# Sliding-window attention feeding a gated MLP: probabilities times values in plain float32, and GpSimd's subtractions and ScalarE's scalings moved to VectorE

## The chip, the cores and the metric

The kernel runs on one core of one Trainium2 chip. The metric is device time in microseconds (us) of one launch. Engines are named as in the profile: PE is TensorE's matmul, PEld its weight load, DVE is VectorE, ACT is ScalarE, POOL is GpSimd, SP is SyncE, which issues most of the DMAs.

## The reference

Three stages follow each other. Attention has batch 2, 8 heads, 768 positions and head size 64, a window of 128 positions and 4 sink positions; the result is laid out as 1536 tokens by 512 channels and goes through a two-layer MLP of width 2048. The third stage applies top-1 experts to the tokens whose score `x @ w_skip` is positive.

```
scores = where(is_sink | in_window, q @ k.T / sqrt(D), -1e9)
a = exp(scores - max);  a = a / (sum(a) + 1e-9);  attn = a @ v
h = x @ w_in
g = where(h >= 1, h, where(h <= -1, 0, (h + 1)**2 / 4))
x = g @ w_out
out = x;  out[x @ w_skip > 0] += gate * (relu(xc @ w1[e]) @ w2[e])
```

With the inputs used here no token has a positive score, so the kernel reads the weights of no expert and ends after a test of the scores. The MLP's weights come as float64 and are turned into float32 in the kernel.

## The kernel before, in words

**Precision.** Most products run on float32r, a rounded float32. To keep float32 accuracy each operand is split into a high part (rounded to float32r) and a low part (what the rounding left, by a subtraction), and a product is the sum of three matmuls: high times high, low times high, high times low. This holds for the scores, for probabilities times values, and for both layers of the MLP.

**Attention.** The work is cut into 48 units, in the order batch, group of 256 queries (3 per batch), head; two neighbouring heads are a pair, of which there are 24. Eight pairs lie in a first group (g = 0) and have no sinks of their own; the other 16 do. For a unit, `score` (line 385) makes the masked scores of two tiles of 128 queries in PSUM, takes their maximum on DVE (line 397) and the exponential with its sum on ACT (line 401). `norm` (line 406) adds 1e-9 to the sums on POOL (line 410), takes the reciprocal on DVE (line 411), and scales the first tile on ACT (line 418) and the second on DVE (line 416). `ptrans` (line 429) turns the blocks of 128 by 128 on PE into PSUM (line 443; 3 blocks where g = 0, else 4), from which ACT writes the high part `pth` (line 448) and DVE the low part `ptl` (line 449). `av` (line 460) multiplies them with the values of the pair and adds the sinks' share; ACT and DVE then write the high and low parts of the result (lines 485 and 486).

**Values.** `load_v` (line 289) loads the values of four heads into `vn` through SP's queue; `split_v` (line 310) splits them per pair into `vst`, which holds three blocks of 128 keys: the high part by ACT for the first 4 pairs (line 317), by DVE for the other 20 (line 319), the low part by POOL for all 24 (line 320). The matmuls of a pair at line 480 are these:

```
mm = [(1, 0, 256, 0), (2, 128, 128, 2)]                    # g == 0
mm = [(1, 0, 256, 0), (2 or 0, 0, 128, 2), (0 or 2, 128, 128, 3)]
for kb, c0, w, i0 in mm:
    for x, pp in ((0, pthp), (1, pthp), (0, ptlp)):
        todo.append((oj[:, :, c0:c0 + w], vs[:, x, kb], pp[:, :, ...]))
```

Each covers both heads of the pair, so w = 256 is a matmul of 512 columns and w = 128 one of 256 columns.

**MLP.** A unit of the MLP is 256 tokens by 256 hidden channels: 24 matmuls of 256 columns (`h_mm`, line 493), the activation (`h_act`, lines 505 to 529: ACT, ACT, DVE, ACT, and the low part `gl` on an engine given by the caller), and 12 matmuls of 512 columns (`y_mm`, line 531). 15 units run beside the attention in pieces; the rest follow in `behind` (line 582). Weights are converted by `conv` (line 201): three or more bit operations on DVE (lines 172 to 174), the high part on ACT (line 180), the low part by `lower` (line 183). 12 conversions are made by `conv` beside the attention, with the low part on POOL, the other 20 in `behind`, with the low part on DVE.

**Order.** In the attention the order on PE is written out by hand: for each step `s_` a string such as `aq.A.k.bPs.` (line 722) says when scores (a, b), transposes of q, k and probabilities (q, k, P, s), probabilities times values (A) and MLP pieces (a dot) go. The order on the other queues is chosen by a planner at build time. In `behind` the order of all engines is written by hand. Of queues, SP carries the loads of q, k, v and of the raw weights, the swaps of halves of the transposed queries (lines 349 and 350) and the partial results.

Of the kernel before, what the change touches and what calls it, by code (L numbers as in the profile page):

```python
# [8 lines left out]
F32 = mybir.dt.float32  # L9
F32R = mybir.dt.float32r  # L10
# [14 lines left out]
def attention_moe_skip_kernel(  # L25
# [15 lines left out]
    nc = tc.nc  # L41
# [72 lines left out]


    kts = [ap.tile([P, 3 * (P + SK)], F32R, name=f"kt{h}", bufs=1) for h in range(H)]
    vst = [ap.tile([P, 2, 3, P], F32R, name=f"vst{i}", bufs=1) for i in range(NP)]
    pcs = [ap.tile([P, 2, 72], F32R, name=f"pc{i}", bufs=1) for i in range(2)]
    ones = const.tile([P, 1], F32, name="ones")
    nc.vector.memset(ones, 1.0)  # L120
# [80 lines left out]
    def conv(w, f, wp, ranged):  # L201
        t = wp.tile([P, 2, 512], F32R, name="wi" if w == 0 else "wo")
        cf = bits(raws.pop((w, f)), ranged)
        upper(cf, t[:, 0])
        lower(cf, t[:, 0], t[:, 1], nc.gpsimd)
        (woh if w else wih)[f] = t


# [56 lines left out]
    natqk, natv, pr_, st = {}, {}, [dict() for _ in range(NPR)], [dict() for _ in range(NU)]  # L265

    def geo(n):

# [18 lines left out]
        natqk[m] = (qn, kn)  # L287

    def load_v(m):
        b, g, h0, kbs, _ = geo(4 * m)  # L290
        vn = ap.tile([P, 2, 4, D], F32, name="vn")
        for t in range(2):
            r = kbs[t] * P
            nc.sync.dma_start(vn[:, t], v[b, h0:h0 + 4, r:r + P, :].rearrange("h p d -> p h d"))
        natv[m] = vn

    def split_qk(u):
        qn, kn = natqk[u // 2]
# [11 lines left out]
    def split_v(u):  # L310
        b, g, h, kbs, s0 = geo(2 * u)
        vn = natv[u // 2]
        i = 2 * (u % 2)
        vs = vst[h // 2]
        vv = vs.rearrange("p x k (j d) -> p x k j d", j=2)[:, :, s0:s0 + 2]
        if u < 4:
            nc.scalar.activation(vv[:, 0], vn[:, :, i:i + 2], AF.Copy)
        else:
            nc.vector.tensor_copy(vv[:, 0], vn[:, :, i:i + 2])
        nc.gpsimd.tensor_tensor(out=vv[:, 1], in0=vn[:, :, i:i + 2], in1=vv[:, 0].bitcast(F32), op=ALU.subtract)  # L320
        pr_[u].update(vs=vs)
# [84 lines left out]
    def norm(n):  # L406
        g = units[n][1]
        pr, lsum = st[n]["pr"], st[n]["lsum"]
        rs = ap.tile([P, 2], F32, name="rs", bufs=3)
        nc.gpsimd.tensor_scalar(out=rs, in0=lsum, scalar1=1e-9, scalar2=None, op0=ALU.add)  # L410
        nc.vector.reciprocal(rs, rs)  # L411
        for t in range(2):
            w = span_of(n, t)[1]
            a, r = pr[:, t, :w], rs[:, t:t + 1]
            if t:
                nc.vector.tensor_scalar(out=a, in0=a, scalar1=r, scalar2=None, op0=ALU.mult)  # L416
            else:
                nc.scalar.activation(a, a, AF.Copy, scale=r)
        if g:

            j = SK * (n % 2)
            pc = pcs[n // 2 % 2]
            dst = pc.rearrange("p t (x c) -> p t x c", x=9)[:, :, 0::8, j:j + SK]
            src = pr[:, :, P:P + SK]
            nc.gpsimd.tensor_copy(dst, src.unsqueeze(2).to_broadcast([P, 2, 2, SK]))
            nc.gpsimd.tensor_tensor(
                out=pc[:, :, 32 + j:32 + j + SK], in0=src, in1=pc[:, :, j:j + SK].bitcast(F32), op=ALU.subtract)

    def ptrans(n):

        g = units[n][1]
        pr = st[n]["pr"]
        lo_, hi_ = 0, P + SK
        if g == 0:
            blocks = [(0, 0), (1, lo_), (1, hi_)]
        elif g % 2:
            blocks = [(0, lo_), (1, hi_), (0, hi_), (1, lo_)]
        else:
            blocks = [(0, hi_), (1, lo_), (0, lo_), (1, hi_)]
        w = len(blocks) * P  # L440
        pt = pst.tile([P, 512], F32, name="pt")
        for i, (t, c) in enumerate(blocks):
            nc.tensor.transpose(pt[:, P * i:P * i + P], pr[:, t, c:c + P], ident)  # L443
        pr = pr_[n // 2]
        if n % 2 == 0:
            pr.update(pth=ap.tile([P, 2, 512], F32R, name="pth", bufs=1), ptl=ap.tile([P, 2, 512], F32R, name="ptl", bufs=1))
        pth, ptl = pr["pth"][:, n % 2, :w], pr["ptl"][:, n % 2, :w]
        nc.scalar.activation(pth, pt[:, :w], AF.Copy)  # L448
        nc.vector.tensor_tensor(out=ptl, in0=pt[:, :w], in1=pth.bitcast(F32), op=ALU.subtract)  # L449
# [9 lines left out]

    def av(u):  # L460
        b, g, h, _, _ = geo(2 * u)
        vs = pr_[u]["vs"]
# [10 lines left out]
        pthp, ptlp = pr_[u]["pth"], pr_[u]["ptl"]  # L473
        for kb, c0, w, i0 in mm:
            for x, pp in ((0, pthp), (1, pthp), (0, ptlp)):
                todo.append((oj[:, :, c0:c0 + w], vs[:, x, kb], pp[:, :, i0 * P:i0 * P + w]))
        if g:
            todo.append((oj, vsk[b][:, h // 2], psk[0:72].unsqueeze(1).to_broadcast([72, 2, 256])))
        for i, (out_, lhs, rhs) in enumerate(todo):
            nc.tensor.matmul(out_, lhs, rhs, start=(i == 0), stop=(i == len(todo) - 1))  # L480
        gi = b * NG + g
        hp = h // 2
        for j in range(2):
            r = slice(D * j, D * j + D)
# [160 lines left out]

# [51 lines left out]
    with tc.manual_schedule(engines={mybir.EngineType.PE}):  # L697
        for s_ in range(-1, NU + 1):
# [25 lines left out]
            for what in order:  # L724
                if what == ".":
                    a, b = np_ * dot // dots, np_ * (dot + 1) // dots
                    dot += 1
                    for i in range(b - a):
                        pieces[done["piece"]]()
                        done["piece"] += 1  # L730
                elif what == "q":
                    upto("tq", done["tq"] + 1, NPR, trans_q)
                elif what == "k":
                    if s_ >= 0:
                        upto("tk", done["tk"] + 1, NU, lambda n: trans_k(n // 2, n % 2))
# [149 lines left out]
    def general_mlp(gp):  # L885
# [5 lines left out]
        for f in range(0, NF, 2):  # L891
# [154 lines left out]
```

## Time and profile before

| | |
|---|---|
| median of 3 runs | 446.63 us (445.97 to 447.99) |
| the profiled execution's own time | 449.18 us |
| its span, first to last instruction | 447.4 us |
| mean granted TensorE clock | 0.943 of full |
| PE / PEld busy | 393.0 (88%) / 354.1 (79%) us |
| DVE / ACT / POOL busy | 328.6 (73%) / 261.0 (58%) / 101.4 (23%) us |
| attention and the MLP beside it | 0 to 246 us |
| MLP alone | 246 to about 439 us |

The profile has one execution. A group is the instructions of one line, engine and shape, with the mean duration of one. A matmul's duration is a model and neighbouring matmuls overlap in it: what one really costs in a row of matmuls is read from the difference of start times. The chain of work that ended last is followed back from the last instruction, at each step to what released it. Of a SyncE wait the profile names the engine that released it last.

### The profile page before, as it was taken

The numbers are of one execution on the slowest core, as the hardware profiler recorded it, in microseconds if no ns is written. First come the engines' busy times: TensorE is split into PE (matmuls) and PEld (weight loads), VectorE is DVE, ScalarE is ACT, GpSimd is POOL, SyncE is SP. The second block draws the span as 40 slices with busy tenths as digits, with TensorE's granted clock in tenths as the row PEclk, the third lists the DMA queues.
The fourth block names the chain that finished last, engine by engine and source line by source line (L and its number), as shares of the span: only waits on it lengthen the run. The fifth ranks groups of instructions, "written<-read, shape, count | busy, mean of one in ns | idle before, by whom it ended". The sixth has DMA issues, their size and how long they took to land.

```text
span 447.4 us, 7553 instructions
## 1 busy us (share of the span) xinstructions
PE 393.0 (88%) x2476; PEld 354.1 (79%) x2476; DVE 328.6 (73%) x823; ACT 261.0 (58%) x625; POOL 101.4 (23%) x223
## 2 busy tenths in 40 slices
PE   4576566999899989999999999999999999999970
PEld 4565465998788878888889979999999999999950
DVE  6999999467788878888885689878854875444452
ACT  3766656688788869898797455444433333333310
POOL 6386566334322323233222000000000000000000
PEclk9966669899999989999999999999999999999995
DMA  6796575322424334241120256544325896555131
GB/s 152 206 282 164 142 211 144 92 50 47 120 48 95 106 87 96 53 112 25 26 72 5 66 188 206 181 132 142 111 79 188 284 347 217 189 188 189 47 141 58
DMA packets 69089, 59.12 MB, mean 132 GB/s; under 512 B 41008, under 2 KB 57392, under 8 KB 69040
## 3 DMA queue, kind: packets, MB, share of 16 engines
q1 hardware_dynamic: 67952, 58.28, 44.5%
q8 instruction: 22, 0.36, 0.4%
q10 hardware_dynamic: 1088, 0.26, 0.3%
q14 instruction: 27, 0.22, 0.2%
HBM read 46.47 MB, written 6.29 MB: 118 GB/s over the span
## 4 chain that ended last, share of the span: by engine, by line
PE 62%; DVE 17%; ACT 9%; issue 5%; DMA 3%; POOL 2%; ACTq 0%; POOLq 0%; DVEq 0%; SPq 0%
PE ph L500 15%; PE y L545 13%; PE z L545 12%; PE pt L500 10%; PE pt L480 5%; PE sc L395 3%; ACT pr L401 2%; DVE xl L486 2%; PE pt L443 2%; DVE cc L174 2%; DVE pr L397 2%; DVE ptl L449 1%; DVE pr L416 1%; DVE cc L173 1%; ACT pth L448 1%
## 5 line engine op out<-in xcount | busy, mean ns | idle before, releaser
L500 PE MATMUL ph<-xh,wi 128*128 128x256 f32 x496 | 93.3, 288 | 3.1 <-DVE rs L411 2.8
L500 PEld LDWEIGHTS ph<-xh,wi 128*128 128x128 f32 x496 | 79.1, 193 | 5.7 <-issue 3.0
L545 PE MATMUL y<-wo,gh 128*128 128x512 f32 x224 | 71.5, 400 | 1.2 <-ACT mr L564 1.2
L500 PE MATMUL ph<-xl,wi 128*128 128x256 f32 x248 | 70.9, 286 | 1.7 <-DVE xl L486 1.7
L500 PEld LDWEIGHTS ph<-xl,wi 128*128 128x128 f32 x248 | 48.4, 195 | 2.3 <-DVE xl L486 2.3
L395 PE MATMUL sc<-kt,qt 128*128 128x260 f32 (+1 forms) x192 | 47.0, 336 | 3.6 <-DMA qt<-qt 2.3
L401 ACT ACTIVATE pr<-pr,negmax 128x260 f32<-128x260 f32 (+1 forms) x96 | 46.7, 487 | 5.3 <-DVE negmax L397 4.3
L522 ACT ACTIVATE gh<-mt 128x512 fp32r<-128x512 f32 x48 | 30.3, 631 | 33.1 <-PE z L545 13.2
L545 PE MATMUL z<-wo,gh 128*128 128x512 f32 x160 | 49.2, 389 | 0.0
L500 PE MATMUL pt<-xh,wi 128*128 128x256 f32 x272 | 48.8, 281 | 0.0
L545 PEld LDWEIGHTS y<-wo,gh 128*128 128x128 f32 x224 | 39.7, 190 | 7.7 <-ACT mr L564 1.4
L545 PE MATMUL y<-wo,gl 128*128 128x512 f32 x112 | 43.9, 392 | 0.0
L500 PEld LDWEIGHTS pt<-xh,wi 128*128 128x128 f32 x272 | 42.7, 188 | 1.3
L395 PEld LDWEIGHTS sc<-kt,qt 128*128 128x128 f32 x192 | 35.2, 222 | 6.1 <-issue 1.9
L528 DVE TENSOR_TENSOR gl<-mt,gh 128x512 fp32r<-128x512 f32 x33 | 22.9, 693 | 23.1 <-ACT gh L522 23.0
L514 ACT ACTIVATE mt<-ph,half 128x512 f32<-128x512 f32 x31 | 21.3, 687 | 31.3 <-PE ph L500 31.2
L443 PE MATMUL pt<-ident,pr 128*128 128x128 f32 x176 | 30.9, 294 | 9.1 <-ACT kt L376 3.9
L500 PE MATMUL pt<-xl,wi 128*128 128x256 f32 x136 | 38.2, 281 | 0.0
L449 DVE TENSOR_TENSOR ptl<-pt,pth 128x512 fp32r<-128x512 f32 (+1 forms) x48 | 30.9, 643 | 7.7 <-ACT pth L448 7.2
L520 DVE SCALAR_TENSOR_TENSOR mt<-ph,mt 128x512 f32<-128x512 f32 x31 | 21.3, 688 | 18.6 <-ACT mt L515 16.9
L480 PE MATMUL pt<-pth,vst 128*128 128x256 f32 (+1 forms) x128 | 34.1, 356 | 0.0
L545 PEld LDWEIGHTS z<-wo,gh 128*128 128x128 f32 x160 | 28.8, 188 | 4.9
(119 smaller groups left out, 833.0 us busy)
## 6 DMA issues: line engine op xcount, KB each, us to landing
raw<-in_moe_w_in_dram SPq DMA_DIRECT2D x32, 512.0 KB, 4.5
raw<-in_moe_w_out_dram SPq DMA_DIRECT2D x32, 512.0 KB, 4.0
qt<-qt SPq DMA_DIRECT2D x44, 128.0 KB, 2.4
vn<-in_v_dram SPq DMA_DIRECT2D x24, 128.0 KB, 3.2
ypart<-mr SPq DMA_DIRECT2D x12, 256.0 KB, 3.0
yi<-ypart SPq DMA_DIRECT2D x12, 256.0 KB, 4.3
out_dram<-mr SPq DMA_DIRECT2D x12, 256.0 KB, 2.0
qn<-in_q_dram SPq DMA_DIRECT2D x22, 128.0 KB, 2.5
```

Of the source, the lines that this page charges most:

```text
L174: nc.vector.scalar_tensor_tensor(out=c, in0=L_, scalar=29, in1=c, op0=ALU.logical_shift_right, op1=ALU.bitwise_or)
L395: nc.tensor.matmul(sc[:, :w], qt[:, x, n % 2, P * t:P * t + P], kts[h][:, c0:c0 + w], start=(x == 0), stop=(x == 1))
L401: nc.scalar.activation(pr[:, t, :w], pr[:, t, :w], AF.Exp, bias=negmax[:, mi:mi + 1], scale=-1.0, accum_out=lsum[:, t:t + 1],)
L443: nc.tensor.transpose(pt[:, P * i:P * i + P], pr[:, t, c:c + P], ident)
L449: nc.vector.tensor_tensor(out=ptl, in0=pt[:, :w], in1=pth.bitcast(F32), op=ALU.subtract)
L480: nc.tensor.matmul(out_, lhs, rhs, start=(i == 0), stop=(i == len(todo) - 1))
L500: nc.tensor.matmul(ph, wih[f + i][:, wx, c * P:c * P + P], xx[gi][:, c], start=(c == 0 and x == 0), stop=(c == KC - 1 and x == 2),)
L514: nc.scalar.activation(t, ph, AF.Relu, bias=half, scale=0.5)
L520: nc.vector.scalar_tensor_tensor(out=t, in0=ph, scalar=1.0, in1=t, op0=ALU.max, op1=ALU.min)
L522: nc.scalar.activation(gh, t, AF.Copy)
L528: eng.tensor_tensor(out=gl, in0=t, in1=gh.bitcast(F32), op=ALU.subtract)
L545: nc.tensor.matmul(ycur[gi, tt], gg[:, c:c + P], woh[f + i][:, wx], start=(u == us[0] and i == 0 and x == 0), stop=(u == us[-1] and i == 1 ...
```

## The change

Probabilities and values are no longer split. `load_v` writes the loaded values straight into one float32 tile `vall`, which holds three blocks of keys for all heads of a batch; `split_v` and `vst` go. `ptrans` writes one float32 tile `pth` (two buffers instead of one) and no `ptl`. `av` issues one float32 matmul for each block where three float32r ones stood; the sinks' matmul stays as it was. Both tiles of a unit are scaled on DVE. The low parts of the 12 conversions beside the attention and of the 15 MLP units there are made on DVE instead of POOL. POOL keeps the addition of 1e-9, the small copies of the sinks' columns, and the subtractions for q and k of six pairs (line 307). A last hunk passes VectorE instead of GpSimd in the path for other inputs, which isn't run here.

```
--- before.py
+++ after.py
@@ -114,7 +114,7 @@
 
 
     kts = [ap.tile([P, 3 * (P + SK)], F32R, name=f"kt{h}", bufs=1) for h in range(H)]
-    vst = [ap.tile([P, 2, 3, P], F32R, name=f"vst{i}", bufs=1) for i in range(NP)]
+    vall = ap.tile([P, 3, H, D], F32, name="vall", bufs=1)
     pcs = [ap.tile([P, 2, 72], F32R, name=f"pc{i}", bufs=1) for i in range(2)]
     ones = const.tile([P, 1], F32, name="ones")
     nc.vector.memset(ones, 1.0)
@@ -202,7 +202,7 @@
         t = wp.tile([P, 2, 512], F32R, name="wi" if w == 0 else "wo")
         cf = bits(raws.pop((w, f)), ranged)
         upper(cf, t[:, 0])
-        lower(cf, t[:, 0], t[:, 1], nc.gpsimd)
+        lower(cf, t[:, 0], t[:, 1], nc.vector)
         (woh if w else wih)[f] = t
 
 
@@ -262,7 +262,7 @@
     units = [(b, g, h) for b in range(B) for g in range(NG) for h in range(H)]
     NU = len(units)
     NPR = NU // 2
-    natqk, natv, pr_, st = {}, {}, [dict() for _ in range(NPR)], [dict() for _ in range(NU)]
+    natqk, pr_, st = {}, [dict() for _ in range(NPR)], [dict() for _ in range(NU)]
 
     def geo(n):
 
@@ -287,12 +287,10 @@
         natqk[m] = (qn, kn)
 
     def load_v(m):
-        b, g, h0, kbs, _ = geo(4 * m)
-        vn = ap.tile([P, 2, 4, D], F32, name="vn")
+        b, g, h0, kbs, s0 = geo(4 * m)
         for t in range(2):
             r = kbs[t] * P
-            nc.sync.dma_start(vn[:, t], v[b, h0:h0 + 4, r:r + P, :].rearrange("h p d -> p h d"))
-        natv[m] = vn
+            nc.sync.dma_start(vall[:, s0 + t, h0:h0 + 4], v[b, h0:h0 + 4, r:r + P, :].rearrange("h p d -> p h d"))
 
     def split_qk(u):
         qn, kn = natqk[u // 2]
@@ -306,19 +304,6 @@
             nc.vector.tensor_copy(s_[:, :, :, 0], n_[:, :, i:i + 2])
             eng.tensor_tensor(out=s_[:, :, :, 1], in0=n_[:, :, i:i + 2], in1=s_[:, :, :, 0].bitcast(F32), op=ALU.subtract)
         pr_[u].update(qs=qs, ks=ks)
-
-    def split_v(u):
-        b, g, h, kbs, s0 = geo(2 * u)
-        vn = natv[u // 2]
-        i = 2 * (u % 2)
-        vs = vst[h // 2]
-        vv = vs.rearrange("p x k (j d) -> p x k j d", j=2)[:, :, s0:s0 + 2]
-        if u < 4:
-            nc.scalar.activation(vv[:, 0], vn[:, :, i:i + 2], AF.Copy)
-        else:
-            nc.vector.tensor_copy(vv[:, 0], vn[:, :, i:i + 2])
-        nc.gpsimd.tensor_tensor(out=vv[:, 1], in0=vn[:, :, i:i + 2], in1=vv[:, 0].bitcast(F32), op=ALU.subtract)
-        pr_[u].update(vs=vs)
 
     def whole(u):
 
@@ -412,10 +397,7 @@
         for t in range(2):
             w = span_of(n, t)[1]
             a, r = pr[:, t, :w], rs[:, t:t + 1]
-            if t:
-                nc.vector.tensor_scalar(out=a, in0=a, scalar1=r, scalar2=None, op0=ALU.mult)
-            else:
-                nc.scalar.activation(a, a, AF.Copy, scale=r)
+            nc.vector.tensor_scalar(out=a, in0=a, scalar1=r, scalar2=None, op0=ALU.mult)
         if g:
 
             j = SK * (n % 2)
@@ -443,10 +425,8 @@
             nc.tensor.transpose(pt[:, P * i:P * i + P], pr[:, t, c:c + P], ident)
         pr = pr_[n // 2]
         if n % 2 == 0:
-            pr.update(pth=ap.tile([P, 2, 512], F32R, name="pth", bufs=1), ptl=ap.tile([P, 2, 512], F32R, name="ptl", bufs=1))
-        pth, ptl = pr["pth"][:, n % 2, :w], pr["ptl"][:, n % 2, :w]
-        nc.scalar.activation(pth, pt[:, :w], AF.Copy)
-        nc.vector.tensor_tensor(out=ptl, in0=pt[:, :w], in1=pth.bitcast(F32), op=ALU.subtract)
+            pr.update(pth=ap.tile([P, 2, 512], F32, name="pth", bufs=2))
+        nc.scalar.activation(pr["pth"][:, n % 2, :w], pt[:, :w], AF.Copy)
 
     def ptrans_sinks(u):
         if units[2 * u][1] == 0:
@@ -459,7 +439,6 @@
 
     def av(u):
         b, g, h, _, _ = geo(2 * u)
-        vs = pr_[u]["vs"]
         o = pst.tile([P, 512], F32, name="pt")
 
 
@@ -470,10 +449,10 @@
         else:
             mm = [(1, 0, 256, 0), (2 if g % 2 else 0, 0, 128, 2), (0 if g % 2 else 2, 128, 128, 3)]
         todo = []
-        pthp, ptlp = pr_[u]["pth"], pr_[u]["ptl"]
+        pth = pr_[u]["pth"]
         for kb, c0, w, i0 in mm:
-            for x, pp in ((0, pthp), (1, pthp), (0, ptlp)):
-                todo.append((oj[:, :, c0:c0 + w], vs[:, x, kb], pp[:, :, i0 * P:i0 * P + w]))
+            vs = vall[:, kb, h:h + 2].rearrange("p j d -> p (j d)")
+            todo.append((oj[:, :, c0:c0 + w], vs, pth[:, :, i0 * P:i0 * P + w]))
         if g:
             todo.append((oj, vsk[b][:, h // 2], psk[0:72].unsqueeze(1).to_broadcast([72, 2, 256])))
         for i, (out_, lhs, rhs) in enumerate(todo):
@@ -633,13 +612,13 @@
             u += 1
 
 
-    done = dict(p=0, ps=0, av=0, qk=0, v=0, sqk=0, sv=0, tq=0, tk=0)
+    done = dict(p=0, ps=0, av=0, qk=0, v=0, sqk=0, tq=0, tk=0)
 
 
     def p_h(u, i, cs):
         h_mm(u, i, (psh, "ph"), cs)
         if i and cs[-1] == KC - 1:
-            h_act(u, nc.gpsimd)
+            h_act(u, nc.vector)
 
     pieces = []
 
@@ -737,8 +716,6 @@
                     score(s_ + 1, "ab".index(what))
                     if what == "b":
                         norm(s_ + 1)
-                        if s_ >= 0 and s_ % 2 == 0:
-                            upto("sv", s_ // 2 + 1, NPR, split_v)
                 elif what == "P":
                     upto("p", s_ + (s_ >= LAG), NU, ptrans)
                 elif what == "s":
```

## Rows read from the trace of the kernel before

**Rows 1.** Busy time by stretch: start:end, length, each engine, clock, DMA.
```profile
20.00:80.00 60.00, 38.56 (x178) 33.65 (x179) 56.91 (x139) 37.32 (x97) 39.19 (x53) 0.70 0.68 186
80.00:230.00 150.00, 141.25 (x948) 126.66 (x948) 118.59 (x353) 123.73 (x344) 47.06 (x120) 0.98 0.29 73
230.00:246.00 16.00, 16.00 (x111) 14.55 (x110) 9.85 (x27) 12.39 (x30) 3.56 (x12) 1.00 0.02 4
```

**Rows 2.** Chain that ended last, 20 to 80 us, shares by line.
```profile
by line: issue 14.1%; DVE cc L174 11.9%; DVE cc L173 7.3%; PE pt L480 6.4%; DVE ptl L449 5.8%; ACT pr L401 5.5%; PE ph L500 4.8%; DVE xl L486 3.9%; DVE cc L172 3.4%; PE sc L395 3.2%; DVE pr L416 2.9%; DVE pr L397 2.9%; DVE qs L306 2.8%; POO
```

**Rows 3.** The same chain, 80 to 230 us: shares, then pieces (start, length).
```profile
by line: PE ph L500 12.0%; PE y L545 10.5%; PE pt L480 9.5%; PE sc L395 5.7%; issue 5.4%; ACT pr L401 4.5%; DVE xl L486 4.4%; PE pt L443 4.1%; DVE kt L369 2.9%; ACT pth L448 2.7%; DVE pr L397 2.7%; DVE pr L416 2.6%; DVE vst L319 2.4%; ACT m
...
124.37 0.60 DVE ptl L449
...
130.26 1.35 DVE vst L319
...
173.38 0.50 ACT pr L418
...
202.06 1.36 DVE vst L319
...
215.28 0.69 DVE ptl L449
...
218.54 0.52 ACT pr L418
```

**Rows 4.** VectorE groups, 20 to 80 us: count, busy, mean ns, idle.
```profile
L174 DVE SCALAR_TENSOR_TENSOR cc<-raw,cc 128x512 uint32<-128x512 uint32 x13 | 11.0, 845 | 0.0
L173 DVE SCALAR_TENSOR_TENSOR cc<-raw,cc 128x512 uint32<-128x512 uint32 x12 | 10.5, 874 | 0.2
...
L319 DVE CAST vst<-vn 128x256 fp32r<-128x256 f32 x5 | 5.0, 1002 | 1.0 <-PE pt L480 1.0
...
L449 DVE TENSOR_TENSOR ptl<-pt,pth 128x384 fp32r<-128x384 f32 x6 | 3.3, 550 | 0.1
L449 DVE TENSOR_TENSOR ptl<-pt,pth 128x512 fp32r<-128x512 f32 x4 | 2.7, 681 | 0.0
```

**Rows 5.** GpSimd group, 20 to 80 us.
```profile
L183 POOL TENSOR_TENSOR wi<-cc,wi 128x512 fp32r<-128x512 f32 x6 | 8.7, 1452 | 3.4 <-ACT wi L180 3.4
```

**Rows 6.** VectorE groups after 246 us, GpSimd idle.
```profile
L528 DVE TENSOR_TENSOR gl<-mt,gh 128x512 fp32r<-128x512 f32 x33 | 22.9, 693 | 23.1 <-ACT gh L522 23.0
...
L173 DVE SCALAR_TENSOR_TENSOR cc<-raw,cc 128x512 uint32<-128x512 uint32 x19 | 13.2, 693 | 0.7
...
L183 DVE TENSOR_TENSOR wi<-cc,wi 128x512 fp32r<-128x512 f32 x10 | 6.8, 684 | 0.0
```

**Rows 7.** Line 416: duration ns min/median/max.
```profile
L416 DVE TENSOR_SCALAR pr<-pr,rs x48: 339/356/1437, 13.9 to 239.2; 128x260 f32<-128x260 f32 x48
```

**Rows 8.** TensorE in order of time, 235 to 240.5 us.
```profile
235.83 0.63 PE L480 MATMUL pt<-pth,vst 128*128 128x512 f32 x2
...
236.53 0.40 PE L480 MATMUL pt<-pth,vst 128*128 128x256 f32 x2
...
237.24 0.40 PE L480 MATMUL pt<-psk,vsk 72*128 72x512 f32 x1
...
238.86 0.60 PE L443 MATMUL pt<-ident,pr 128*128 128x128 f32 x4
239.22 0.70 PE L545 MATMUL y<-wo,gh 128*128 128x512 f32 x2
```

**Rows 9.** TensorE groups, 80 to 230 us: transposes, and one for each pair.
```profile
L443 PE MATMUL pt<-ident,pr 128*128 128x128 f32 x120 | 19.3, 278 | 0.9 <-ACT pr L418 0.4 <-DVE pr L416 0.4
...
L480 PE MATMUL pt<-ptl,vst 128*128 128x512 f32 x17 | 6.7, 395 | 0.0
```

**Rows 10.** The one plain float32 matmul call of the program, line 786.
```profile
L786 PE MATMUL pt<-todo,ones x2: 182/182/182, 439.5 to 439.5; 128*1 128x13 f32 x2
```

**Rows 11.** SyncE queue waits of the loads of v (total, times, longest).
```profile
SPq L294 <- POOL rs L410: 8.3, 3, 5.1
```

More of the change, by code (lines that the diff above doesn't have):

```diff
@@ L116, in attention_moe_skip_kernel @@
     kts = [ap.tile([P, 3 * (P + SK)], F32R, name=f"kt{h}", bufs=1) for h in range(H)]
-    vst = [ap.tile([P, 2, 3, P], F32R, name=f"vst{i}", bufs=1) for i in range(NP)]
+    vall = ap.tile([P, 3, H, D], F32, name="vall", bufs=1)
     pcs = [ap.tile([P, 2, 72], F32R, name=f"pc{i}", bufs=1) for i in range(2)]
@@ L204, in conv @@
         upper(cf, t[:, 0])
-        lower(cf, t[:, 0], t[:, 1], nc.gpsimd)
+        lower(cf, t[:, 0], t[:, 1], nc.vector)
         (woh if w else wih)[f] = t
@@ L264, in attention_moe_skip_kernel @@
     NPR = NU // 2
-    natqk, natv, pr_, st = {}, {}, [dict() for _ in range(NPR)], [dict() for _ in range(NU)]
+    natqk, pr_, st = {}, [dict() for _ in range(NPR)], [dict() for _ in range(NU)]
     def geo(n):
@@ L289, in load_v @@
     def load_v(m):
-        b, g, h0, kbs, _ = geo(4 * m)
-        vn = ap.tile([P, 2, 4, D], F32, name="vn")
+        b, g, h0, kbs, s0 = geo(4 * m)
         for t in range(2):
             r = kbs[t] * P
-            nc.sync.dma_start(vn[:, t], v[b, h0:h0 + 4, r:r + P, :].rearrange("h p d -> p h d"))
-        natv[m] = vn
+            nc.sync.dma_start(vall[:, s0 + t, h0:h0 + 4], v[b, h0:h0 + 4, r:r + P, :].rearrange("h p d -> p h d"))
     def split_qk(u):
@@ L308, in split_qk @@
         pr_[u].update(qs=qs, ks=ks)
[L310 to L321, printed above, removed]
     def whole(u):
@@ L414, in norm @@
             a, r = pr[:, t, :w], rs[:, t:t + 1]
[L415 to L418, printed above, removed]
+            nc.vector.tensor_scalar(out=a, in0=a, scalar1=r, scalar2=None, op0=ALU.mult)
         if g:
@@ L445, in ptrans @@
         if n % 2 == 0:
[L446 to L449, printed above, removed]
+            pr.update(pth=ap.tile([P, 2, 512], F32, name="pth", bufs=2))
+        nc.scalar.activation(pr["pth"][:, n % 2, :w], pt[:, :w], AF.Copy)
     def ptrans_sinks(u):
@@ L461, in av @@
         b, g, h, _, _ = geo(2 * u)
-        vs = pr_[u]["vs"]
         o = pst.tile([P, 512], F32, name="pt")
@@ L472, in av @@
         todo = []
-        pthp, ptlp = pr_[u]["pth"], pr_[u]["ptl"]
+        pth = pr_[u]["pth"]
         for kb, c0, w, i0 in mm:
-            for x, pp in ((0, pthp), (1, pthp), (0, ptlp)):
-                todo.append((oj[:, :, c0:c0 + w], vs[:, x, kb], pp[:, :, i0 * P:i0 * P + w]))
+            vs = vall[:, kb, h:h + 2].rearrange("p j d -> p (j d)")
+            todo.append((oj[:, :, c0:c0 + w], vs, pth[:, :, i0 * P:i0 * P + w]))
         if g:
@@ L633, in behind @@
             u += 1
-    done = dict(p=0, ps=0, av=0, qk=0, v=0, sqk=0, sv=0, tq=0, tk=0)
+    done = dict(p=0, ps=0, av=0, qk=0, v=0, sqk=0, tq=0, tk=0)
     def p_h(u, i, cs):
@@ L641, in p_h @@
         if i and cs[-1] == KC - 1:
-            h_act(u, nc.gpsimd)
+            h_act(u, nc.vector)
     pieces = []
@@ L739, in attention_moe_skip_kernel @@
                         norm(s_ + 1)
-                        if s_ >= 0 and s_ % 2 == 0:
-                            upto("sv", s_ // 2 + 1, NPR, split_v)
                 elif what == "P":
@@ L901, in general_mlp @@
                     h_mm(u, i, (psh, "ph"))
-                h_act(u, nc.gpsimd)
+                h_act(u, nc.vector)
                 gh, gl = ms[u]["gh"], ms[u]["gl"]
```

## The prediction

> **What bounds the kernel now.** I first read the busy time of each engine by stretch [rows 1]. Up to 246 us the attention runs with parts of the MLP beside it; from there on the MLP runs alone. Three kinds of stretch are to be seen. From 20 to 80 us DVE is busy 56.91 of 60 us while PE stands near two thirds of the time at a clock of 0.70: DVE is the bound. From 80 to 230 us PE shows 141.25 of 150, but ACT (123.73) and DVE (118.59) are near full as well. From 230 to 246 us PE is busy 16.00 of 16. After 246 us nothing is left that the change touches.
>
> Then I read the chain that ended last. From 20 to 80 us its largest items are DVE's bit operations on the raw weights, and the low part of the probabilities (L449) has 5.8% [rows 2]. From 80 to 230 us the five largest matmul lines have 12.0, 10.5, 9.5, 5.7 and 4.1%, together 42%; the rest is DVE, ACT and their hand-overs [rows 3]. So PE is not alone in setting the pace there, though it looks 94% busy: the modelled ends of matmuls overlap. The weight loads, one for each matmul, give a better reading. In the stretch where PE never waits they are busy 14.55 of 16 us, 91%; from 80 to 230 us it is 126.66 of 150, 84% [rows 1]. At 91% the same matmuls would take 126.66/0.91 = 139.3 us, so PE has about 10.7 us of slack, and that is what relief of ACT and DVE can win.
>
> **A float32 matmul.** None of this shape is in the trace, so its price is bounded. Three float32r matmuls of 512 columns start over 0.70 us (235.83 to 236.53) and six of 256 over 0.71 (to 237.24), 0.233 and 0.118 each [rows 8]: a pair with sinks pays 1.41 us for its nine, one with g = 0 1.05 for its six. The one plain float32 call of the program, at line 786, appears as two matmuls [rows 10]. If each of the two ran like float32r, a block would cost two thirds of now: 0.94 us, a gain of 0.47 per pair (lower end). The only other float32 matmuls are the transposes: four of 128 columns span 0.60 us, less the 0.278 that one lasts [rows 9] that is three steps of 0.107, or 0.43 for 512 columns; the next instruction starts 0.36 after the first of the four [rows 8], which gives 0.36. Twice 0.43 is 0.86 for 512 columns and 0.43 for 256, so a pair with sinks pays 1.72 and one with g = 0 1.29: +0.31 and +0.24 us. I take this, since it comes from operands of the same type; 0.36 would give +0.03. The Trainium skill ("FP8 and Floating Point Precision", TensorE Precision Notes) says that true float32 takes four passes through the array. By that rule a block costs 4/3 of three passes, +0.47 and +0.35 per pair, and the stretch from 80 to 230 us would pay 7.5 us instead of the 5.0 below; no run so far shows it.
>
> **20 to 80 us.** Removed from DVE: ten L449 (3.3 + 2.7 us) and five L319 (5.0) [rows 4], 11.0 us. Added: twelve low parts of weights at 0.684 us (the duration of the same operation on DVE later), one gl at 0.693 [rows 6], and ten more scalings at 0.356, the median of L416 [rows 7] (half of them are narrower, so this is an upper end): 8.2 + 0.7 + 3.6 = 12.5. By instructions alone DVE gains nothing. But what stays gets shorter: L173 and L174 take 874 and 845 ns here, beside a busy POOL [rows 4], and 693 with POOL idle [rows 6]; 12 x 0.18 + 13 x 0.15 = 4.1 us, and a few tenths on L172, L306 and L416 each. POOL is busy 39.19 us in the stretch; the six wi low parts are 8.7 of it [rows 5], the six of wo about the same, and the values' subtractions go too, so well over half of POOL's work leaves; the q and k subtractions stay. I take three quarters of 6 us, 4.5, and DVE's balance is -11.0 + 12.5 - 4.5 = -3.0 us. As DVE is the bound, I count it in full. PE's longer matmuls run at the low clock, but PE has 21 us to spare here; if that cover failed they would cost about 1 us (6.4% of 60 us [rows 2], a quarter more). Bounds: -6 (all the contention, and POOL's waits in the chain) to +1.5 (none of the contention lifted). Before 20 us the same items nearly cancel.
>
> **80 to 230 us.** PE: 17 pairs [rows 9], of which four have g = 0 (the second batch's): 13 x 0.31 + 4 x 0.24 = +5.0 us. ACT loses the scalings, two for each pair at 0.5 us [rows 3], 34 x 0.5 = 17 us at most: 82% busy becomes about 72%. DVE loses 34 L449 (8 of 0.55 us, 26 of 0.68 [rows 4], 22 us) and the other 15 of the 20 L319, and gains 34 scalings at 0.356 and 14 gl at 0.693, 21.8 us: its 79% falls by a few points. In the chain itself L449 stands four times (first 0.60, last 0.69) and L418 four times (first 0.50, last 0.52), and two L319 of 1.35 and 1.36 us [rows 3]; an L319 or L416 has no reason of its own to last so long (L416: 356 ns median, 1437 at most [rows 7]), and such long ones lie beside a POOL subtraction. So work of about 2.2 + 2.0 + 2.7 us leaves the chain directly. Other paths stand close behind, so not all of PE's slack comes back: I take three quarters of the 10.7 us, 8.0. The balance is 5.0 - 8.0 = -3.0 us. Bounds: +5.0 (no slack recovered) to -5.7 (all of it). Next in line when L449 is gone: the ACT copy of the probabilities (L448), and behind it PE itself.
>
> **230 to 246 us.** PE is full; two pairs with sinks, +0.6 us, nothing to set against it.
>
> **Costed at nothing.** The first four ACT copies of values (ACT is idle there). A second buffer of pth. The loads of v: same number and size, but each now waits until PE has read the slot for the same heads of the group before; until now it waited for a buffer that POOL had to read, and SP's queue stood behind POOL for it (8.3 us in three waits [rows 11]). Queued on SP behind such a load stand the query swaps, which the scores wait for. By the order in the code that last reading is in the step before the load's, and a swap comes more than a pair of units ahead of its scores, which covers a delay of a step; if that cover failed, ten loads would cost up to a few us. After 246 us nothing changes.
>
> **Sum.** -3.0 - 3.0 + 0.6 = -5.4 us: 449.2 becomes 443.8. The profiled execution lies 2.6 us above the median of 446.63, so the forecast for a median is 441.2 us. A measurement of this kernel can tell about 0.5% (2.2 us) from no change.
>
> **Rivals.**
> 1. *PE is the bound.* The added matmul time is paid in full, and relief of DVE and ACT meets a PE that has no room: 80 to 230 us costs +5.0, the next stretch +0.6, and the early one is even: 452.2 us. For it: PE busy 141.25 of 150 and an order written by hand, in which a longer block pushes all that follows. Against it: 42% of the chain. With the early stretch even, it decides as soon as less than 3.4 of the 10.7 us come back. By the rule of four passes above the time would be 455. Chance 0.22.
> 2. *All the slack comes back.* -6 early and -5.7 + 0.6 later: 435.5 us. For it: weight loads at 84%. The Trainium skill ("Perfetto Trace Analysis", Identifying the Most-Contended Engine) says that a tensor engine's headroom is read from weight-load share, not from matmul share. By it the slack is 16% of 150, 24 us, of which the full stretch's own 9% can't be had. Chance 0.20.
> 3. *The gains and losses cancel.* DVE gets 48 scalings and 27 subtractions and, in the early stretch, no relief from POOL because the q and k subtractions stay: 0 early, -0.4 later, +0.6: 446.8 us. Chance 0.16.
>
> The forecast has 0.42. Faster by over 0.5% is the forecast with rival 2: 0.62; within 0.5% 0.16; slower 0.22. The range is from 434.5 (rival 2, a little beyond) to 451.0, which leaves out about 0.05 below and the upper half of rival 1.
>
> **What would show it.** Right: L449, L319, L320 and L418 gone; L480 with two matmuls a call starting 0.43 us apart for 512 columns; L416 near 0.36 us with few beyond 0.5; L173 near 0.70 before 80 us; the first MLP matmul of the attention phase and the end of the attention each about 3 and 5 us earlier; ACT near 72% in the middle. Wrong: float32 matmuls dearer than 0.43 us per 512 columns and half, PE weight loads or starts with no gaps in the middle stretch while the time has grown, L173 still at 0.85, or scores waiting for a swap behind a load of v.

## The result, and the profile after

The changed kernel takes 434.38 us (433.54 to 435.37, 4 runs) against 447.31 for the kernel before in the same comparison: ratio 0.971, 95% interval [0.968, 0.975]. It is faster, as forecast, but by 12.9 us where 5.4 were forecast, and it lies just outside the range (434.5 to 451.0). Its profiled execution took 433.92 us with a span of 432.1.

Busy time by stretch of the changed kernel, columns as in [rows 1]:

```profile
20.00:80.00 60.00, 47.27 (x233) 37.64 (x233) 53.99 (x159) 39.06 (x105) 21.65 (x42) 0.83 0.68 188
80.00:230.00 150.00, 144.55 (x927) 124.95 (x926) 107.67 (x360) 114.22 (x318) 22.64 (x94) 1.00 0.29 72
230.00:246.00 16.00, 14.73 (x100) 13.21 (x100) 11.38 (x20) 8.76 (x16) 0.00 (x0) 1.00 0.28 90
```

Against [rows 1], more operations of every engine but POOL are done by 80 us: PE has 233 matmuls in the first stretch where it had 178. The attention ends near 231 us instead of 246, so the last stretch is already the MLP alone.

To see where the time was won, stretches have to begin and end at the same work. The mark used from here on is the first matmul of probabilities times values of a pair. The fifth pair is at 65.66 us before and 56.50 after, the sixth at 82.26 and 71.31, the last (the 24th) at 242.72 and 228.74. So 10.95 us are won before the sixth pair, 3.0 from there to the last, and about 1.3 behind it. Together that is 15.3 us, the difference of the two profiled executions, where the medians differ by 12.9; in which stretch the rest of 2.4 us lies can't be told. A mark comes from one execution: the same kernel profiled twice has the sixth pair at 71.31 and 69.96, another at 68.63 and 71.02, so this mark is good to some 2.4 us. The time from it to the last pair came out as 157.43 and 157.71, and as 155.18 and 154.79, so it is good to about 0.4 us.

Up to the sixth pair the changed kernel has this row (start:end, length, then as in [rows 1]):

```profile
0.00:71.31 71.31, 49.90 (x223) 39.84 (x223) 64.20 (x199) 41.97 (x115) 27.65 (x73) 0.86 0.71 189
```

VectorE's groups up to the sixth pair, first before, then after (line numbers shift: L306 is L304, L416 is L400 in the changed kernel):

```profile
L173 DVE SCALAR_TENSOR_TENSOR cc<-raw,cc 128x512 uint32<-128x512 uint32 x13 | 11.2, 860 | 0.2
L174 DVE SCALAR_TENSOR_TENSOR cc<-raw,cc 128x512 uint32<-128x512 uint32 x13 | 11.0, 845 | 0.0
L172 DVE TENSOR_SCALAR cc<-raw 128x512 uint32<-128x512 uint32 x13 | 6.8, 526 | 0.0
L416 DVE TENSOR_SCALAR pr<-pr,rs 128x260 f32<-128x260 f32 x13 | 5.7, 442 | 0.1
...
L306 DVE CAST ks<-kn 128x256 fp32r<-128x256 f32 x9 | 4.3, 475 | 0.2 <-PE pt L374 0.2
```

```profile
L173 DVE SCALAR_TENSOR_TENSOR cc<-raw,cc 128x512 uint32<-128x512 uint32 x13 | 8.9, 686 | 0.1
L174 DVE SCALAR_TENSOR_TENSOR cc<-raw,cc 128x512 uint32<-128x512 uint32 x12 | 8.2, 682 | 0.1
L400 DVE TENSOR_SCALAR pr<-pr,rs 128x260 f32<-128x260 f32 x18 | 6.8, 401 | 0.1
L183 DVE TENSOR_TENSOR wi<-cc,wi 128x512 fp32r<-128x512 f32 x6 | 5.5, 923 | 0.1
L172 DVE TENSOR_SCALAR cc<-raw 128x512 uint32<-128x512 uint32 x13 | 5.4, 417 | 0.0
...
L304 DVE CAST ks<-kn 128x256 fp32r<-128x256 f32 x9 | 2.5, 282 | 0.0
L400 DVE TENSOR_SCALAR pr<-pr,rs 128x128 f32<-128x128 f32 x8 | 2.2, 278 | 0.0
```

Several operations that the change leaves alone are shorter by a fifth to two fifths: L173 860 to 686 ns, L172 526 to 417, the copies of k 475 to 282. The wide scalings shrink less (442 to 401).

The float32 matmuls in order of time in the changed kernel, and the end of the same work before, which continues [rows 8]:

```profile
221.54 1.88 PE L459 MATMUL pt<-pth,vall 128*128 128x512 f32 x6
223.07 0.59 PE L459 MATMUL pt<-psk,vsk 72*128 72x512 f32 x1
223.50 0.40 PE L479 MATMUL ph<-xh,wi 128*128 128x256 f32 x2
```

```profile
237.48 0.40 PE L500 MATMUL ph<-xh,wi 128*128 128x256 f32 x2
```

A pair with sinks takes 221.54 to 223.50, 1.96 us, where it took 235.83 to 237.48, 1.65: +0.31 us. All calls of the 24 pairs show as two matmuls each, 64 calls and 128 matmuls:

```profile
L459 PE MATMUL pt<-pth,vall x128: 378/379/1162, 23.8 to 230.2; 128*128 128x256 f32 x80, 128*128 128x512 f32 x48
```

### The profile page after: what moved, and what is told of

Read it like the earlier page. It is cut to its first block, busy times and chain, and to the rows that moved or that the text cites. A ratio compares the mean times of both kernels' runs of the same rounds, so it can differ in the third digit from the quotient of the medians.

```text
span 432.1 us, 7260 instructions
## 1 busy us (share of the span) xinstructions
PE 391.6 (91%) x2412; PEld 343.5 (80%) x2412; DVE 306.7 (71%) x830; ACT 240.7 (56%) x573; POOL 52.1 (12%) x172
## 4 chain that ended last, share of the span: by engine, by line
PE 70%; DVE 16%; ACT 4%; DMA 4%; issue 3%; POOL 1%; SPq 1%; ACTq 0%; DVEq 0%; POOLq 0%
PE ph L479 18%; PE y L524 15%; PE z L524 11%; PE pt L479 10%; PE pt L459 7%; PE sc L380 4%; PE pt L425 3%; DVE pr L400 2%; DMA qt<-qt 2%; DVE pr L382 2%; DVE cc L173 1%; DVE cc L174 1%; DVE mt L499 1%; ACT pr L386 1%; DVE xl L465 1%
## 5 line engine op out<-in xcount | busy, mean ns | idle before, releaser
L479 PE MATMUL ph<-xh,wi 128*128 128x256 f32 x496 | 92.3, 286 | 3.8 <-DVE mt L499 3.8
L479 PEld LDWEIGHTS ph<-xh,wi 128*128 128x128 f32 x496 | 78.1, 190 | 6.9 <-DVE mt L499 3.2
L479 PE MATMUL ph<-xl,wi 128*128 128x256 f32 x248 | 70.0, 282 | 0.9 <-DVE xl L465 0.9
L507 DVE TENSOR_TENSOR gl<-mt,gh 128x512 fp32r<-128x512 f32 x48 | 33.1, 690 | 25.6 <-ACT gh L501 25.3
L380 PE MATMUL sc<-kt,qt 128*128 128x260 f32 (+1 forms) x192 | 45.7, 327 | 3.5 <-DMA qt<-qt 2.7
L459 PE MATMUL pt<-pth,vall 128*128 128x256 f32 (+1 forms) x128 | 46.4, 498 | 0.0
L380 PEld LDWEIGHTS sc<-kt,qt 128*128 128x128 f32 x192 | 33.8, 213 | 6.2 <-DMA qt<-qt 2.9
L459 PEld LDWEIGHTS pt<-pth,vall 128*128 128x128 f32 x128 | 24.6, 207 | 14.3 <-issue 13.4
L425 PE MATMUL pt<-ident,pr 128*128 128x128 f32 x176 | 30.0, 291 | 6.0 <-DVE pr L400 4.8
```

Source lines behind the costliest of these rows:

```text
L380: nc.tensor.matmul(sc[:, :w], qt[:, x, n % 2, P * t:P * t + P], kts[h][:, c0:c0 + w], start=(x == 0), stop=(x == 1))
L479: nc.tensor.matmul(ph, wih[f + i][:, wx, c * P:c * P + P], xx[gi][:, c], start=(c == 0 and x == 0), stop=(c == KC - 1 and x == 2),)
L507: eng.tensor_tensor(out=gl, in0=t, in1=gh.bitcast(F32), op=ALU.subtract)
```

## The experiments

The kernels of the study in one table; a series on the scalings follows at the end. The ratio is to the kernel before on the same chip (its median was 446.2 to 447.3 us). The next columns are from the profiled execution: start of the sixth pair, VectorE's busy time until then, and the time from the sixth pair to the last.

| kernel | median us | ratio, 95% interval | sixth pair | DVE busy | sixth to last |
|---|---|---|---|---|---|
| before | 446.2 to 447.3 | 1 | 82.26 | 72.38 | 160.5 |
| changed | 434.38 | 0.971 [0.968, 0.975] | 71.31 | 64.20 | 157.4 |
| a: float32 matmuls only | 435.93 | 0.977 [0.975, 0.979] | 74.78 | 64.80 | 153.7 |
| b: low parts to DVE only | 441.56 | 0.988 [0.986, 0.990] | 76.58 | 69.17 | 158.5 |
| c: scalings to DVE only | 444.94 | 0.997 [0.995, 0.998] | 82.40 | 76.44 | 156.5 |
| d: changed, weights' low parts on POOL | 441.95 | 0.991 [0.988, 0.994] | 78.34 | 69.22 | 158.0 |
| e: changed, one scaling on ACT | 430.65 | 0.967 [0.961, 0.972] | 68.63 | 60.55 | 155.2 |
| f: changed, MLP low parts on POOL | 433.40 | 0.970 [0.965, 0.975] | 71.56 | 63.85 | 157.4 |
| g: a, both splits as dead work | 447.13 | 1.001 [0.998, 1.003] | 80.07 | 71.51 | 161.8 |
| h: before, extra matmuls early | 444.56 | 0.996 [0.993, 0.998] | 80.69 | 69.77 | 158.7 |
| i: a, weights' low parts on DVE | 430.57 | 0.967 [0.963, 0.971] | 70.61 | 61.30 | 154.2 |
| j: a, probabilities' low part as dead work | 443.80 | 0.993 [0.989, 0.996] | 80.95 | 69.47 | 158.1 |
| k: a, values' split as dead work | 443.36 | 0.995 [0.992, 0.997] | 78.70 | 67.78 | 158.8 |
| l: e, q and k low parts on DVE | 431.84 | 0.965 [0.959, 0.972] | 72.65 | 61.67 | 155.3 |

### Which part won the time: a, b, c, d

Each of a, b and c makes one part of the change in the kernel before; d undoes one part in the changed kernel.

```diff
 # a: the changed kernel with norm's two branches, and nc.gpsimd in conv and p_h, as before
 # b: the kernel before with
-        lower(cf, t[:, 0], t[:, 1], nc.gpsimd)
+        lower(cf, t[:, 0], t[:, 1], nc.vector)
-            h_act(u, nc.gpsimd)
+            h_act(u, nc.vector)
 # c: the kernel before with both scalings on nc.vector
 # d: the changed kernel with
-        lower(cf, t[:, 0], t[:, 1], nc.vector)
+        lower(cf, t[:, 0], t[:, 1], nc.gpsimd)
```

> The kernel before with only the float32 matmuls: values read as loaded, probabilities not split. The scaling of the first tile stays on ScalarE, the low parts of the 12 weights and the 15 MLP units stay on GpSimd. Theory V (the work of the two splits, L449 and the values' halves on VectorE and GpSimd, was what held the first 65 us): most of the 12.9 us comes here, 436 to 440 us, and the fifth pair's probabilities times values start at 57 to 60 us (before 65.7, after 56.5). Theory L (GpSimd's long subtractions, which stretch VectorE's operations beside them and hold the small ones queued behind): little comes here, 444 to 447 us, fifth pair at 63 to 65, and L173 still at 0.85 us before 80 us.

> The kernel before with only the low parts of the 12 weights and of the 15 MLP units moved from GpSimd to VectorE. Theory L: most comes here, 437 to 440 us, fifth pair at 57 to 60 us, L173 at 0.70. Theory V: VectorE gets 9 us more work in its full stretch, 446 to 452 us, fifth pair at 65 to 70.

> The kernel before with only both scalings on VectorE. Both theories: VectorE is full before 80 us, so 446 to 450 us; a gain of over 2 us here would mean that ScalarE's load in the middle stretch (82%) was what counted.

> The changed kernel with the low parts of the 12 weights back on GpSimd. Theory L: it gives back most of the early gain, 440 to 444 us, L173 back at 0.80 or more. Theory V: VectorE has 8 us less to do in its full stretch, 431 to 435 us.

Measured: a won 10.4 us (446.36 to 435.93), most of the whole, as theory V had it, and this with L173 no shorter than before up to the sixth pair:

```profile
L173 DVE SCALAR_TENSOR_TENSOR cc<-raw,cc 128x512 uint32<-128x512 uint32 x13 | 12.7, 980 | 0.1
```

But b won 4.8, between what the two theories expected, though it only adds work to VectorE, which theory V had as a loss; and d gave back 7.6 us, as theory L had it. Both mechanisms are real. c, where no gain was expected, won 1.4 us, under the 2 us that would have spoken for ScalarE's load. The two rows up to the sixth pair, of b and of d (the columns are start:end, length, PE, PEld, DVE, ACT, POOL, clock, DMA):

```profile
0.00:76.58 76.58, 52.57 (x233) 46.18 (x234) 69.17 (x205) 47.80 (x133) 35.89 (x82) 0.79 0.71 193
```

```profile
0.00:78.34 78.34, 52.36 (x222) 42.90 (x223) 69.22 (x189) 42.57 (x116) 43.99 (x85) 0.83 0.70 185
```

In b VectorE does 205 operations by the sixth pair where it did 192 before, and is busy 69.17 us instead of 72.38. In d, with POOL's subtractions back, L173 has become longer again:

```profile
L174 DVE SCALAR_TENSOR_TENSOR cc<-raw,cc 128x512 uint32<-128x512 uint32 x13 | 12.3, 943 | 0.1
L173 DVE SCALAR_TENSOR_TENSOR cc<-raw,cc 128x512 uint32<-128x512 uint32 x13 | 12.2, 937 | 0.1
L172 DVE TENSOR_SCALAR cc<-raw 128x512 uint32<-128x512 uint32 x13 | 8.0, 613 | 1.4 <-DMA raw<-in_moe_w_in_dram 1.4
...
L400 DVE TENSOR_SCALAR pr<-pr,rs 128x128 f32<-128x128 f32 x8 | 4.3, 532 | 0.0
```

All of them are VectorE operations that the two kernels share: 24.5 us for L173 and L174 in d, 17.1 for one operation less in the changed kernel. With L172 (8.0 for 5.4), the narrow scalings (4.3 for 2.2) and smaller ones, the subtractions on POOL lengthen VectorE's other work by some 12 us, more than the 8.9 that they cost on VectorE itself. In b, the copy of values (L319), of which [rows 4] have a mean of 1002 ns, is back at 308.

That it is GpSimd's subtractions can be seen operation by operation in the trace of the kernel before. Of the 132 operations of L173, L174, L319 and L416, 14 take more than 1 us, and each of the 14 runs beside a GpSimd subtraction. Of those that meet no subtraction of over 0.6 us, the longest takes 694 ns for L173 and L174, 308 for L319 and 459 for L416. Two of the pairs, VectorE's operation and then GpSimd's (start, length):

```profile
40.73 1.44 DVE L173 SCALAR_TENSOR_TENSOR cc<-raw,cc 128x512 uint32<-128x512 uint32 x1
40.35 1.27 POOL L183 TENSOR_TENSOR wo<-cc,wo 128x512 fp32r<-128x512 f32 x1
...
202.06 1.36 DVE L319 CAST vst<-vn 128x256 fp32r<-128x256 f32 x1
201.99 1.28 POOL L528 TENSOR_TENSOR gl<-mt,gh 128x512 fp32r<-128x512 f32 x1 [0.91 <-ACT gh L522]
```

### Work or clock: g and h

In a the granted clock between 20 and 56 us was 0.91, before 0.65. So the longer float32 matmuls could have helped by keeping the clock up. g keeps them and puts the removed work back, as dead work; h keeps the old work and adds matmuls.

```diff
 # g: a, with
+        nc.vector.tensor_tensor(out=pr["ptl"][:, n % 2, :w], in0=pt[:, :w], in1=pth, op=ALU.subtract)
+    def split_v(u): ...   # as before, from vall into a tile that nothing reads
 # h: the kernel before, in av
+        if u < 5:
+            for _ in range(4):
+                nc.tensor.matmul(*todo[0], start=True, stop=True)
```

> The kernel with only the float32 matmuls (435.9 us), with the work of both splits put back as dead work: the same subtractions and copies on VectorE, ScalarE and GpSimd, into tiles that nothing reads. Theory W (the early gain of that kernel is the work taken off VectorE and GpSimd): the fifth pair's probabilities times values start at 63 to 66 us again, the total is 443 to 448 us. Theory C (TensorE's clock, granted 0.91 of full between 20 and 56 us in that kernel and 0.65 before, is kept up by the longer float32 matmuls, and is the gain): clock still about 0.9 there, fifth pair at 57 to 60 us, 436 to 440 us.

> The kernel before with four more matmuls of 512 columns ahead of those of each of the first five pairs (into the same place, overwritten): TensorE has more to do there and nobody has less. Theory C: the clock between 20 and 56 us rises to 0.85 or more and the fifth pair starts earlier, 58 to 63 us, total 439 to 444 us. Theory W: the clock may rise, but VectorE sets the pace, fifth pair at 65 to 69 us, total 446 to 451 us.

The rows from 20 to 56 us of the kernel before, a, g and h:

```profile
20.00:56.00 36.00, 22.67 (x96) 19.83 (x96) 34.88 (x94) 22.26 (x60) 24.30 (x35) 0.65 0.70 189
20.00:56.00 36.00, 23.99 (x114) 18.12 (x115) 34.44 (x90) 24.54 (x70) 26.56 (x35) 0.91 0.73 205
20.00:56.00 36.00, 22.23 (x81) 16.51 (x82) 35.01 (x92) 21.35 (x60) 23.43 (x30) 0.73 0.67 188
20.00:56.00 36.00, 23.50 (x103) 19.45 (x103) 33.38 (x91) 21.06 (x58) 24.17 (x32) 0.86 0.72 203
```

g takes 447.13 us, ratio 1.001 [0.998, 1.003]: with the removed work back, nothing of a's gain is left. Its fifth pair comes at 64.86 us, and its clock is 0.73 though it has the longer matmuls. What these cost by themselves g can't say exactly, as no instruction waits for the dead work. In h the clock rose as wanted, but the fifth pair stayed at 66.33 us:

```profile
0.00:80.69 80.69, 54.92 (x254) 46.43 (x255) 69.77 (x191) 48.41 (x132) 52.03 (x95) 0.87 0.69 187
```

```profile
0.00:82.26 82.26, 51.65 (x234) 45.66 (x234) 72.38 (x192) 48.75 (x132) 50.55 (x95) 0.77 0.69 183
```

(h, then before.) A clock of 0.87 instead of 0.77 goes with 1.6 us of 82, less than the spread of the mark. The total of h is 1.8 us below the kernel before (446.35 to 444.56), which theory W had not expected (446 to 451 us). So a higher clock may be worth up to about 2 of a's 10.4 us; the rest is the work, and the clock mainly followed the gain. Theory W holds in the main.

### Which half of the splits: j and k

```diff
 # j: a with the dead subtraction of g alone;  k: a with the dead split_v of g alone
```

> The kernel with only the float32 matmuls (435.9 us), with the subtraction for the low part of the probabilities put back on VectorE as dead work (48 times, 0.55 to 0.69 us), the values' split left out. If VectorE's own work is the larger part of what the split cost: 441 to 445 us, fifth pair at 60 to 64 us. If the values' split with its GpSimd subtractions is: 436 to 440 us, fifth pair at 57 to 59.

> The same kernel with the values' split put back as dead work instead (20 copies on VectorE, 24 subtractions on GpSimd), the probabilities' low part left out. The two alternatives the other way round: 436 to 439 us and fifth pair at 57 to 59 us if VectorE's own work is the larger part, 441 to 445 us and 60 to 64 us if GpSimd's subtractions with what waits beside them are.

Neither is the larger part: j gives back 7.9 us and k 7.4, each more than half of the 11.2 of both together. By the sixth pair j has 4.7 us more of VectorE's work than a, k 3.0. k has few operations on VectorE and 24 subtractions on POOL. By the table, what the splits cost is not paid early alone: from the sixth pair to the last j takes 4.4 us more than a, k 5.1 and g 8.1, and up to the sixth pair 6.2, 3.9 and 5.3. That the two do not add up is in line with an order that the planner makes anew for every kernel, and it was not tried with one fixed order.

### The scalings: e, i, l, f and a series on one chip

```diff
 # e: the changed kernel with norm as before (one scaling on ACT, one on DVE)
 # i: e with nc.gpsimd in p_h;   l: e with eng = nc.vector in split_qk;   f: the changed kernel with nc.gpsimd in p_h
```

> The changed kernel with the first tile's scaling back on ScalarE and the MLP units' low parts back on GpSimd: of the change only the float32 matmuls and the 12 weights' low parts on VectorE. If the early gain adds up from the two (9.5 us at the fifth pair by the first, 4.4 by the second) and the middle stretch is best with VectorE least loaded (the first alone took 153.7 us from the sixth pair to the last, the whole change 157.4): 429 to 433 us, faster than the whole change, sixth pair at 71 to 73 us. If the scalings belong with the weights' low parts on VectorE (an order that the planner finds only so): 435 to 438 us.

> The changed kernel with the first tile's scaling back on ScalarE. If VectorE's load in the middle stretch costs the 3.7 us there: 431 to 434 us, the time from sixth to last pair 154 to 156 us. If it is the 15 low parts of the MLP units that cost it: 434 to 436 us and 157 us.

> The changed kernel with the first tile's scaling on ScalarE (430.7 us), and the last long subtractions of GpSimd, those of q and k for six pairs, on VectorE too. If GpSimd's long operations still stretch VectorE's in the first 60 us (L173 at 0.72 instead of 0.69): 427 to 430 us. If VectorE's added work (12 of 0.42 us in its full stretch) weighs as much: 430 to 434 us.

> The changed kernel with the 15 low parts of the MLP units back on GpSimd, both scalings on VectorE. If the scalings alone cost the changed kernel the 3.8 us that it has over the kernel with one of them on ScalarE: 433 to 436 us. If GpSimd's subtractions now meet twice as many scalings on VectorE, each of which waits for them: 436 to 440 us, with scalings of more than 1 us in the middle stretch.

e and i are at 430.6, 3.8 us below the changed kernel. So the gains of a and b add up in the whole (10.4 and 4.8 against 15.8 in i), nearly so up to the sixth pair (7.5 and 5.7 against 11.7) and less up to the fifth (9.5 and 4.4 against 10.0); and moving a scaling to VectorE costs. The MLP's 15 low parts make no difference that shows (f against the changed kernel, i against e), and neither do the q and k subtractions (l; L173 fell to 0.68 us, but VectorE got the work). To settle the scalings, a series on one chip had none, one and both of a unit's scalings on VectorE:

```diff
 # m_scale0:  nc.scalar.activation(a, a, AF.Copy, scale=r) for both t;  m_scale1: as e;  m_scale2: the changed kernel
```

> The changed kernel with both scalings of a unit on ScalarE, none on VectorE. If VectorE's load is what counts everywhere: 427 to 430 us, sixth pair at 66 to 69 us. If ScalarE becomes the next bound in the middle stretch (it would have 17 us more than with one scaling, some 95% of 150): 431 to 436 us, sixth pair at 66 to 69 us, but 157 us or more from there to the last pair.

> The changed kernel with one scaling on ScalarE and one on VectorE, on the same chip as its two neighbours: 429 to 432 us, sixth pair at 68 to 69 us, 155 us from there to the last pair, whichever reason holds.

> The changed kernel itself, on the same chip as the two with fewer scalings on VectorE: 433 to 436 us, sixth pair at 71 us, 157 us from there to the last pair. If it is within 1 us of the one with a scaling on ScalarE, the 3.8 us between them was chips or executions, not the scaling.

Medians 433.36, 431.39 and 434.47 us; ratios 0.972 [0.969, 0.975], 0.965 [0.960, 0.969] and 0.974 [0.971, 0.978]. One on each engine is best; its interval doesn't touch that of the changed kernel and ends where that of none begins. The sixth pair is within 1.1 us in all three (69.92, 71.02, 69.96); from there to the last pair, none, one and both:

```profile
69.92:227.04 157.12, 153.79 (x977) 132.37 (x976) 92.93 (x305) 144.92 (x403) 21.33 (x99) 1.00 0.29 73
```

```profile
71.02:225.81 154.79, 152.55 (x977) 132.01 (x976) 104.29 (x342) 132.51 (x368) 22.71 (x99) 1.00 0.31 78
```

```profile
69.96:227.67 157.71, 151.93 (x978) 131.76 (x976) 112.88 (x378) 119.95 (x334) 24.55 (x100) 1.00 0.32 80
```

With none, ACT is busy 144.92 of 157.12 us (92%). With both, neither engine is so full (DVE 72%, ACT 76%), but PE stands idle 5.8 us instead of the 2.2 with one, and its waits for VectorE are 4.4 us instead of 0.9 (total, times, longest):

```profile
PE ph L479 <- DVE mt L499: 2.4, 3, 0.9
...
PE pt L318 <- DVE kt L354: 1.1, 2, 0.6
PE ph L479 <- DVE xl L465: 0.9, 1, 0.9
```

At the end with none, a full ScalarE is the likely limit, but not shown to be all of it: PE's waits for it are 1.3 us against 0.4 with one, and PE is idle 3.3 us against 2.2, where the stretch is 2.3 us longer. At the other end it is single operations of VectorE that come late; that these stand behind the added scaling in VectorE's queue is likely, but was not tried by itself.

## Why the prediction was wrong

**What bounds the kernel.** Right in the main: up to the sixth pair VectorE sets the pace. In every kernel of the table the sixth pair comes 6 to 12 us after VectorE's busy time until then. It is not exact: in c VectorE has 4.1 us more to do, and the sixth pair comes no later (82.40 to 82.26), as its idle time shrinks.

**A float32 matmul.** Right: two matmuls a call, and +0.31 us for a pair with sinks, forecast +0.31, from the transposes. By the four passes of the Trainium skill ("FP8 and Floating Point Precision", TensorE Precision Notes), an estimate of 4/3 of three passes gave +0.47. The trace doesn't bear this estimate out: the six float32 matmuls and the sinks' one take 1.96 us; if the sinks' one still takes its 0.24 of before, the six take 1.72, and 1.72/1.41 is 1.22, not 1.33. The measured pair lies on the value that the forecast took from the transposes.

**20 to 80 us, the step that failed.** The balance was -11.0 + 12.5 - 4.5 = -3.0 us, with a bound of -6. Measured to the sixth pair, by the groups of both kernels: removed 12.1 us (the two L449 before 20 us are in it), added 13.8 (eleven low parts 8.9, as those of wi took 923 ns each; five wide scalings at 0.40 and eight narrow ones at 0.28, 4.2; gl 0.7), and the operations that stayed became 8.3 us shorter, not 4.5: L173 and L174 4.4 for equal counts, L172 1.4, the copies of q and k 2.0, the old scalings 0.5. That makes -6.6; one L174 less by the mark is another 0.7, and VectorE's busy time, without overlaps, fell from 72.38 to 64.20, by 8.2 us. Work removed and added came out as forecast (+1.7 us, forecast +1.5). The term mis-sized is the relief from POOL, 4.5 us where 8.3 were measured: 4.1 us were taken from L173 and L174, which gave 4.4, and a few tenths each from L172, the copies and the scalings, which gave 3.9 together; then a quarter was struck off. Beyond that VectorE's idle time fell by 2.8 us (9.9 to 7.1), which the sum, made of busy time alone, didn't hold. Together 10.95, give or take the 2.4 us of the mark. The relief itself was the right mechanism, as b and d show.

**80 to 230 us.** The sum, -3.0 us, is what was measured between the sixth pair and the last (160.5 to 157.4), but that is luck, since its terms are not what happened. The float32 matmuls with the work they spare win 6.8 us there by themselves (a). PE is busy as long in a as before and loses most of its idle time, 8.8 us before and 1.7 in a (before, then a):

```profile
82.26:242.72 160.46, 151.71 (x1027) 136.10 (x1026) 126.99 (x378) 133.38 (x368) 49.60 (x127) 0.99 0.27 68
74.78:228.47 153.69, 151.96 (x977) 131.89 (x976) 98.55 (x327) 132.98 (x368) 37.58 (x112) 1.00 0.30 75
```

Relief of ScalarE was to win a part of PE's slack too. In the kernel before, the move of the scalings did win 4.0 us there (c); with the splits gone the same move costs 2.9 (the series), so the two reliefs don't add up, and why the sign turns is open. PE's longer matmuls, by the starts 5.3 us for the 18 pairs between these marks, are not seen in PE's busy time, and g, which has them and all the old work, takes 1.3 us more in this stretch. A part may be the granted clock (0.99 before, 1.00 in a); the rest is not explained.

**230 to 246 us, and what was costed at nothing.** +0.6 can't be seen: the stretch behind the last pair became about 1.3 us shorter, in single executions. The loads of v wait for PE now, where they waited for POOL [rows 11]: 13.4 us in 13 waits of SP's queue. PE's waits for the query swaps are 2.7 us in all, before 2.3, so the cover held:

```profile
SPq L293 <- PE pt L459: 13.4, 13, 3.7
```

**The rivals.** The second, all the slack comes back, gave 435.5 us and was within 1.2 us of the measured time; it had 0.20. That too is luck: its terms were -6 early and -5.7 in the middle, and measured were -10.95 and -3.0. By the Trainium skill ("Perfetto Trace Analysis", Identifying the Most-Contended Engine) TensorE's headroom is judged by the weight loads' busy share (or by the share of peak arithmetic), not by that of the matmuls. The traces agree in part: between the marks PE was idle 8.8 us before, and a won 6.8 there with matmuls that ask for 5.3 more by their starts; what the loads' share in a (131.89 of 153.69) would still promise was not tried. The first, PE as the bound, fell: no kernel with the longer matmuls was slower than before by more than can be told. The third, no relief from POOL, fell with the 8.3 us of it.

## What to carry to other kernels

Where one engine sets the pace, count its work between two marks of the same work, and price each of its operations by what it takes with the neighbour quiet; here the lengthening by GpSimd's subtractions was worth more than running them on VectorE. Matmuls that take 0.31 us more a pair, on a TensorE that has slack, were cheaper here than the split that saved this time, since much of the split's work ran on the bound engine or lengthened that engine's operations. Move work off an engine only as far as the balance asks: here the second scaling was one move too many, and the version that leaves it on ScalarE is faster than both kernels, 430.6 to 431.4 us.

## What the runs showed that had not been expected

In the kernel before, every VectorE operation of over 1 us in the four lines looked at lay beside a GpSimd subtraction: bit operations on integers (L173 has a mean of 937 ns in d, 684 in b) as well as copies and scalings (L319 1002 against 308 ns). Operations that read PSUM did not lengthen: L449 is 550 and 681 ns before and 550 and 678 in b. And two pieces of dead work cost 7.9 and 7.4 us alone and 11.2 together.
